# One expert unit of two 64-row halves in plain fp32 in place of two units of 128 rows

## The chip, the cores and the metric

The kernel runs on one core of one Trainium2 chip, in one launch. The metric is the device time of that launch in microseconds (us). A run of a kernel agrees with the next within about 0.3%.

## What is computed

Three layers follow one another; only the second is touched. The attention's output `x` (2304 tokens of 512 numbers) goes to one of eight experts per token, and the result goes through a gated network.

```python
e_idx = np.argmax(x @ w_gate + modality_bias[modality_id], axis=1)
for e in range(8):
    mask = e_idx == e
    h = np.maximum(x[mask] @ w1[e], 0.0)            # 512 -> 1024
    out[mask] = gate_w[mask, None] * (h @ w2[e])    # 1024 -> 512
```

On the reference's own inputs only three experts get tokens: expert 1 gets 48, expert 2 gets 1084 and expert 5 gets 1172. Matmuls keep fp32 accuracy, either as plain fp32 matmuls or as three matmuls of a high and a low part (`hi*hi + hi*lo + lo*hi`) in a type (fp32r) that TensorE streams faster.

## The kernel before

**Stages.** Attention runs first (until about 205 us), then the expert layer in units, then the gated network (from 445.60 us to the end). All engine queues are written out by hand: an engine executes its instructions in the order of the program, and steps of later units are placed between the matmuls of earlier ones.

**Units.** A unit is a set of token rows of one expert. Nine *pair* units (0 to 8, `NA` = 9) of 256 rows come first: two are chosen during the attention (expert 2 twice on these inputs), the other seven by a planner (`Routing.finish`) that counts on the device. What an expert has left, if 128 rows or fewer, goes to *single* units of 128 rows. Here 60 rows of expert 2 and the 48 of expert 1 are left, so units 9 and 10 are singles; both are always in the program. Further singles stand in nested branches (L1848) on the device's count `nb` and aren't taken here.

**The planner.** `finish` compares the counts with the thresholds `thr` on VectorE (L889 to L916), then GpSimd turns the result into the table `tl` (L920 to L940): the expert of each unit, a flag whether it differs from that of the unit before, and `nb`. GpSimd's queue goes on with the scatter of unit 0 (L1212) and the gather of unit 2 (L1105). The sync queue (SP) reads `tl` into registers to address the weight loads.

**Weights.** An expert has eight weight pieces of 512 KB: four column quarters of `w1` (pieces 0, 2, 4, 6) and four row quarters of `w2` (1, 3, 5, 7). Each has one fixed buffer `ws[k]`. `load` (L1122) fills it, and is skipped on the chip where the expert hasn't changed. `high` (L1149, ScalarE) and `low` (L1155, VectorE) split a piece into two fp32r tiles of the pool tag "w" (10 buffers).

**A single unit** (`single`, from L1258) takes 128 rows. `up(q)` makes 256 hidden columns with 12 fp32r matmuls of 256 columns (four chunks of the 512 inputs, three terms; L1272); `turn(q)` transposes them back with two matmuls (L1280) and splits them; `down(q)` adds them to the 512 outputs with six fp32r matmuls of 512 columns (L1288). The plan of eight steps is written out in `plan`. After each step `step` places loads, splits and gathers of the units ahead, and `extra` places work of the gated network: `decode` unpacks its weights (which the inputs hold in a wide format) and stores them to DRAM as `wd`, `early` transposes its first rows (three matmuls, L1525), and `fetch` and `prepare` load and split its first weights.

**Column tiles in the attention.** `Attention.values` (L443) multiplies two heads at once in plain fp32: each matmul has 64 stationary columns, one head writes output partitions 0 to 63 and the other 64 to 127, and the two alternate in the queue.

Of the kernel before, what the change touches and what calls it, by code (L numbers as in the profile page):

```python
# [547 lines left out]
class Routing:  # L548
# [7 lines left out]
    def __init__(self, tc, ctx, keep, xd, ident, mid, w_gate, bias):  # L556
# [10 lines left out]
        self.tl = keep.tile([1, 2 * NU + 1], I32, tag="tl", name="tl")  # L567
# [70 lines left out]
    def tables(self):  # L638
# [24 lines left out]
        self.thr = iota("thr", [P, 2, NA], [[P, 2], [2 * P, NA]])  # L663
# [204 lines left out]
    def finish(self, tmp, ps):  # L868
# [3 lines left out]
        def t(name, shape, dt=F32):  # L872
# [15 lines left out]
        cmp = t("cmp", [P, E, 2, NA])  # L888
        V.tensor_tensor(  # L889
            cmp, cnt.unsqueeze(3).to_broadcast([P, E, 2, NA]), self.thr.unsqueeze(1).to_broadcast([P, E, 2, NA]),  # L890
            ALU.is_gt,
        )
        nu = t("nu", [P, E, 2])
        V.tensor_reduce(nu, cmp, AX.X, ALU.add)
        c = t("c", [P, 2, E])
        V.tensor_copy(c[:, 0], nu[:, :, 1])
        V.tensor_tensor(c[:, 1, ::-1], nu[:, :, 0], nu[:, :, 1], ALU.subtract)
# [9 lines left out]
        V.tensor_scalar(gm, ends, most, None, ALU.min)  # L907
        V.scalar_tensor_tensor(gs, ends, 2.0 * NE, gm, ALU.add, ALU.add)
# [3 lines left out]
            past, self.grp.unsqueeze(2).to_broadcast([P, G, 2 * E]),  # L912
# [3 lines left out]
        V.tensor_reduce(tef, past[0:1], AX.X, ALU.add)  # L916
        yield
        te2 = tef.rearrange("p g o -> p (g o)")
        tl, own, rev = self.tl, t("own", [1, NU]), t("rev", [1, NU])
        g.tensor_copy(own[:, 0:NE], self.te0[:, 0:NE])  # L920
        g.tensor_copy(own[:, NE:NA], te2[:, 2 * NE:2 * NA:2])
        g.tensor_copy(own[:, NA:], te2[:, 2 * NA:])
        g.tensor_scalar(rev, own, -1.0, 2.0 * E - 1, ALU.mult, ALU.add)
        g.tensor_scalar(rev, rev, 0.0, None, ALU.max)
        dif = t("dif", [1, NU])
# [4 lines left out]
        g.tensor_copy(tl[:, 0:NU], own)  # L930
        nb = t("nb", [1, 1])
        g.tensor_scalar(nb, ends[0:1, 2 * E:], float(-2 * (NA - NE)), most[0:1], ALU.add, ALU.add)
        used = t("used", [1, NU])
        g.tensor_scalar(used, self.grp[0:1, 0:NU], float(NA - 1), nb, ALU.subtract, ALU.is_le)
# [5 lines left out]
        g.tensor_copy(tl[:, 2 * NU:], nb)  # L940
# [3 lines left out]
        V.scalar_tensor_tensor(a, gs[:, 0:E], float(P), n0e, ALU.mult, ALU.subtract)  # L944
        V.scalar_tensor_tensor(b, c[:, 0], 2.0 * P, n0e, ALU.mult, ALU.add)
        V.scalar_tensor_tensor(d, c[:, 0], -2.0, gs[:, 2 * E - 1:E - 1:-1], ALU.mult, ALU.add)
# [5 lines left out]
        V.scalar_tensor_tensor(rk, half, float(P), rk, ALU.mult, ALU.add)  # L952
# [17 lines left out]
        V.scalar_tensor_tensor(u[:, 0], gs[:, 0:2 * E], float(-P), co, ALU.mult, ALU.add)  # L970
        V.scalar_tensor_tensor(u[:, 1], gs[:, 0:2 * E], float(P), qf, ALU.mult, ALU.add)
# [17 lines left out]
class Experts:  # L989
# [137 lines left out]
    @staticmethod  # L1127
    def piece(u, p):

        return p if u < NA else (0, 2, 4, 1, 6, 3, 5, 7)[p]  # L1130
# [12 lines left out]
    def high(self, u, p):  # L1143
        k = self.piece(u, p)
        hi = self.w[u, k] = self.part(u, p, "h")
        if (u, p) in self.POOLH:
            self.nc.gpsimd.tensor_scalar(hi, self.ws[k], 1.0, 1.0, ALU.mult, ALU.mult)
        else:
            self.nc.scalar.activation(hi, self.ws[k], AF.Copy)  # L1149

    def low(self, u, p):
        k = self.piece(u, p)
# [6 lines left out]
    def transpose(self, u, c):  # L1159
# [3 lines left out]
        if c == 0:  # L1163
            if u > 1:
# [17 lines left out]
        if u == 1:  # L1182
            if c:
                lo.append(self.ro.wp.tile([P, 2, n], F32R, tag="xg2", name="xl"))
            h, l = hi[c // 2], lo[c // 2]
        else:
            h, l = hi[:, c:c + k], lo[:, c:c + k]
# [70 lines left out]
    def single(self, u, step):  # L1258

        nc = self.nc  # L1260
        xh, xl, _ = self.x[u]
        y = self.ps.tile([P, DM], F32, tag="o", name="y", bufs=1)
        h = {}
        nq = FF // 256

        def up(q):
            wh, wl = self.w[u, 2 * q]
            t = self.ps.tile([P, 2 * P], F32, tag="s", name="h", bufs=SB)
            n = 0
            for c in range(KD):  # L1270
                for a, b in ((xh, wh), (xh, wl), (xl, wh)):
                    nc.tensor.matmul(t, a[:, c, :], b[:, c, :], start=(n == 0), stop=(n == 3 * KD - 1))  # L1272
                    n += 1
            h[q] = self.sp.tile([P, 2 * P], F32, tag="act", name="hr", bufs=5)
            nc.scalar.activation(h[q], t, AF.Copy)

        def turn(q):
# [3 lines left out]
            h[q] = self.relu(t)  # L1281

        def down(q):
            hh, hl = h.pop(q)
            wh, wl = self.w[u, 2 * q + 1]
            for f in range(2):
                for n, (a, b) in enumerate(((hh, wh), (hh, wl), (hl, wh))):
                    nc.tensor.matmul(  # L1288
                        y, a[:, f], b[:, f], start=(q == 0 and f == 0 and n == 0),
                        stop=(q == nq - 1 and f == 1 and n == 2),  # L1290
# [10 lines left out]
    @staticmethod  # L1301
    def ahead(u):

        return u <= NA

    def start(self, u):
        for k in range(8):
            self.load(u, k)
        self.gather(u)
        for p in range(3 + self.ahead(u)):  # L1310
            self.high(u, p)
            if p:
                self.low(u, p - 1)
        for c in range(0, KD, KD // len(self.groups(u))):
            self.transpose(u, c)

    def run(self, units, last, extra):

        for u in units:
            n = u + 1 if u < last else None  # L1320

            def step(f, u=u, n=n):
                for do, a in ((self.low, 2), (self.high, 3)):
                    p = f + a + self.ahead(u)
                    if p < 8:
                        do(u, p)
                    if n is not None and f + a + self.ahead(n) >= 8:
                        do(n, f + a + self.ahead(n) - 8)
                if n is not None:
                    if f == 0:  # L1330
                        if n not in self.g:
                            self.gather(n)
                        self.load(n, self.piece(u, 0))
                        self.load(n, self.piece(u, 1))
                    if f < 6:
                        self.load(n, self.piece(u, f + 2))
# [6 lines left out]
            for _ in (self.pair if u < NA else self.single)(u, step):  # L1343
# [3 lines left out]
class Gated:  # L1347
# [45 lines left out]
    def decode(self, halves=(0, 1)):  # L1393
# [20 lines left out]
        if self.r and (len(self.r) > 1 or not self.todo):  # L1414
# [6 lines left out]
        if self.todo:  # L1421
# [467 lines left out]
```

## Time and profile before

| | us |
|---|---|
| median of 3 runs | 881.71 |
| runs | 881.51 to 881.82 |
| profiled execution, its own time | 881.88 |
| span of its trace | 879.9 |
| TensorE busy in the span | 860.1 |
| VectorE / ScalarE / GpSimd busy | 697.0 / 549.3 / 235.0 |

The span goes from the first to the last instruction, and the profiled execution's own time is 1.98 us longer. In the trace PE is TensorE's matmuls, PEld its weight loads, DVE VectorE, ACT ScalarE, POOL GpSimd and SP the sync engine, of which only the DMA queue matters here. L1272 is line 1272 of the kernel. A matmul's duration contains time in which the next one already runs, so the pace of a series is read from the starts.

### The profile page before, as it was taken

The page shows a single profiled execution, that of the slowest core. Times are in us where ns is not written, and L with a number is a line of the kernel's source. Part 1 is how long each engine was busy: PE and PEld are TensorE (multiplying, and loading weights), DVE is VectorE, ACT ScalarE, POOL GpSimd, SP SyncE. Part 2 cuts the span into 40 slices and gives each one's busy share as a digit, 9 for nine tenths or more (in the row PEclk, how much of TensorE's full clock was granted, in tenths as well). Part 3 has the DMA queues.
Part 4 walks back from the last instruction along what each step waited for, and adds up shares of the span by engine and source line. Part 5 has one row for each costly group of instructions (what it writes and reads, how often), then busy time and mean ns, then how long its engine had stood idle before and what let it go on. Part 6 is the DMA issues. An engine that isn't in the chain of part 4 may idle for free.

```text
span 879.9 us, 16627 instructions
## 1 busy us (share of the span) xinstructions
PE 860.1 (98%) x5536; PEld 747.6 (85%) x5536; DVE 697.0 (79%) x1683; ACT 549.3 (62%) x1190; POOL 235.0 (27%) x482
## 2 busy tenths in 40 slices
PE   7999999999999999999999999999999999999996
PEld 5777767778989999999889988999999999999995
DVE  7677789867989999999789898887666887676751
ACT  7777787774566666667866565556545467545542
POOL 5887876863732222110100000002000002000002
PEclk9999999999999999999999999999999999999998
DMA  7767678964556955579846523234212223321101
GB/s 154 158 146 168 165 170 161 267 152 142 91 157 207 327 175 178 191 235 339 283 148 197 180 85 103 75 106 158 67 64 72 73 73 110 106 72 56 66 1 72
DMA packets 117984, 126.48 MB, mean 144 GB/s; under 512 B 65044, under 2 KB 92200, under 8 KB 117896
## 3 DMA queue, kind: packets, MB, share of 16 engines
q1 hardware_dynamic: 112536, 110.46, 44.1%
q0 software_dynamic: 4640, 14.70, 5.0%
q8 instruction: 44, 0.72, 0.4%
q14 instruction: 44, 0.36, 0.1%
q10 hardware_dynamic: 720, 0.24, 0.1%
HBM read 126.78 MB, written 24.28 MB: 172 GB/s over the span
## 4 chain that ended last, share of the span: by engine, by line
PE 31%; issue 14%; DVE 2%; POOL 1%; ACT 1%; DMA 1%; POOLq 0%; ACTq 0%; DVEq 0%
PE g L1567 20%; PE o L1655 11%; POOL out_dram L1663 1%; PE g L1525 1%; DMA wof<-wd 1%; DVE s L1589 0%; DVE wc L1450 0%; DVE b L1538 0%; DVE ah L1591 0%; DVE x L1554 0%; ACT x L1550 0%; DVE s L1626 0%; ACT pc L1604 0%; DVE wo L1490 0%; POOLq L1884 0%
## 5 line engine op out<-in xcount | busy, mean ns | idle before, releaser
L1567 PE MATMUL g<-x,wc 128*128 128x384 f32 x1524 | 299.1, 338 | 2.8 <-ACT sg L1582 1.2
L1567 PEld LDWEIGHTS g<-x,wc 128*128 128x128 f32 x1524 | 270.6, 188 | 22.6 <-ACT sg L1582 1.5
L1655 PE MATMUL o<-wo,ah 128*128 128x512 f32 x648 | 184.4, 396 | 0.0
L1663 POOL DMA_INDIRECT out_dram<-os,tok x18 | 18.8, 1044 | 408.3 <-ACT os L1662 281.0
L1655 PEld LDWEIGHTS o<-wo,ah 128*128 128x128 f32 x648 | 118.0, 188 | 10.4 <-DVE ah L1591 0.4
L1604 ACT ACTIVATE pc<-g 128x384 f32<-128x384 f32 x102 | 49.9, 489 | 101.0 <-PE g L1567 100.9
L1155 DVE TENSOR_TENSOR wl<-ws,wh 128x1024 fp32r<-128x1024 f32 x76 | 92.2, 1216 | 1.4 <-ACT wh L1149 1.4
L1149 ACT ACTIVATE wh<-ws 128x1024 fp32r<-128x1024 f32 x76 | 80.4, 1061 | 16.3 <-PE y L1242 16.3
L367 ACT ACTIVATE sc<-sc,mn 128x192 f32<-128x192 f32 (+2 forms) x144 | 82.3, 574 | 1.3 <-DVE mn L359 0.8
L299 POOL TENSOR_SCALAR dec<-cum 128x576 f32<-128x576 f32 (+4 forms) x148 | 77.8, 534 | 9.8 <-DMA cum<-drow 5.9
L359 DVE CUSTOM_DVE_ANT_0 sc<-s,dec 128x192 f32<-128x192 f32 (+2 forms) x144 | 58.7, 441 | 20.5 <-POOL dec L299 9.6
L1232 PE MATMUL h<-xh,wh 128*128 128x256 f32 x240 | 69.1, 288 | 0.0
L1232 PE MATMUL h<-xl,wh 128*128 128x256 f32 x240 | 67.8, 283 | 0.0
L1232 PE MATMUL h<-xh,wl 128*128 128x256 f32 x240 | 67.8, 282 | 0.0
L1591 ACT ACTIVATE ah<-s 128x384 fp32r<-128x384 f32 x72 | 37.5, 520 | 43.1 <-DVE s L1589 43.1
L1212 POOL DMA_INDIRECT rows_by_expert<-ys,dst x18 | 21.9, 1214 | 159.1 <-DVE ys L1210 84.6
L350 PE MATMUL s<-qk,qT 64*128 64x320 f32 (+4 forms) x384 | 55.8, 408 | 2.9 <-DVE qk L313 1.6
L1450 DVE TENSOR_TENSOR wc<-wf,wc 128x512 fp32r<-128x512 f32 x72 | 40.2, 560 | 21.3 <-ACT wc L1447 21.3
L350 PEld LDWEIGHTS s<-qk,qT 64*128 64x128 f32 (+1 forms) x384 | 31.2, 177 | 22.6 <-issue 15.8
L1447 ACT ACTIVATE wc<-ws 128x512 fp32r<-128x512 f32 x68 | 42.0, 626 | 10.7 <-DVE ws L1468 8.7
L1242 PE MATMUL y<-wh,hh 128*128 128x512 f32 x120 | 47.6, 397 | 0.7 <-ACT hh L1202 0.7
L1242 PE MATMUL y<-wh,hl 128*128 128x512 f32 x120 | 47.3, 394 | 0.6 <-DVE hl L1203 0.6
(310 smaller groups left out, 1795.8 us busy)
## 6 DMA issues: line engine op xcount, KB each, us to landing
ws<-in_moe_w_dram SPq DMA_DIRECT2D x88, 512.0 KB
wf<-wd SPq DMA_DIRECT2D x36, 512.0 KB
wd<-dec SPq DMA_DIRECT2D x18, 512.0 KB
wof<-wd SPq DMA_DIRECT2D x18, 512.0 KB
cum<-drow SPq DMA_DIRECT2D x15, 576.0 KB
raw<-in_moe_w_gate_dram SPq DMA_DIRECT2D x12, 512.0 KB
raw<-in_moe_w_val_dram SPq DMA_DIRECT2D x12, 512.0 KB
raw<-in_moe_w_out_dram SPq DMA_DIRECT2D x12, 512.0 KB
```

The costliest lines, as they stand in the source:

```text
L299: nc.gpsimd.tensor_scalar(to, c[r, z], -1.0, c[r, a:a + 1], ALU.mult, ALU.add)
L350: nc.tensor.matmul(out[r, o:o + w], q[a, rows], k[a, c:c + w], start=True, stop=True)
L359: nc.vector.tensor_tensor_reduce(s[:, so + c0:so + e], t[j, b, c0][:, 0:e - c0], d[:, do + c0:do + e], -1.0, mn[j][:, 5:6] if c0 else 3.0e ...
L367: nc.scalar.activation(so, so, AF.Exp, bias=mn[j][:, b:b + 1], scale=-1.0, accum_out=sm[:, c:c + 1])
L1149: self.nc.scalar.activation(hi, self.ws[k], AF.Copy)
L1155: eng.tensor_tensor(lo, self.ws[k], hi.bitcast(F32), ALU.subtract)
L1232: nc.tensor.matmul(t, a[:, c, cs], self.chunk(b, c), start=(n == 0), stop=(n == 3 * KD - 1))
L1242: nc.tensor.matmul(y[j], a[:, cs], b[:, f % 2, :], start=(f == 0 and n == 0), stop=(f == nf - 1 and n == 2))
L1447: nc.scalar.activation(t["w"][:, 0, to], of(), AF.Copy)
L1567: self.nc.tensor.matmul(t, p[:, c, :], q[:, c, :], start=(first and n == 0), stop=(n == total - 1), skip_group_check=not first)
L1604: nc.scalar.activation(c, t, AF.Copy)
L1655: nc.tensor.matmul(o[0], x[:, cs], y[:, r, :], start=(o[1] == 0 and k == 0), stop=(o[1] == 2 * self.NP - 1 and k == 2))
```

## The change

Thresholds are now in steps of 64 rows, and what is left of an expert is given out in halves of 64 rows. One unit of 128 rows takes two halves, A on rows 0 to 63 and B on rows 64 to 127, each with an expert of its own. `single` becomes `twin`: each half is a 64-column tile of TensorE, in plain fp32, with no split of weights, inputs or hidden values. The weights of A are read from `ws` itself; those of B come by `load_b` into eight buffers of the tag "w", issued in the last four steps of unit 8. Only unit 9 stands outside the branches; unit 10 and on are taken when `nb`, now in halves, is over 2. `decode` loads no new piece in the last four steps of unit 8 (two are loaded at the end of unit 9 instead), and `fetch` of the gated network's first weights moves from unit 10 to unit 7. The table `tl` gets the experts of the B halves.

```diff
-        self.thr = iota("thr", [P, 2, NA], [[P, 2], [2 * P, NA]])
+        self.thr = iota("thr", [P, 3, NA], [[D, 3], [2 * P, NA]])
+        for j in range(2):
+            nc.gpsimd.iota(
+                self.grp2[D * j:D * (j + 1)], [[2, G]], base=j, channel_multiplier=0, allow_small_or_imprecise_dtypes=True
+            )
...
+        V.tensor_tensor(nu[:, :, 0], nu[:, :, 0], nu[:, :, 1], ALU.add)
+        V.scalar_tensor_tensor(c[:, 1, ::-1], nu[:, :, 2], -2.0, nu[:, :, 0], ALU.mult, ALU.add)
...
+        V.scalar_tensor_tensor(
+            odd, self.grp2[0:1, 2 * NA:].unsqueeze(2).to_broadcast([1, NB, 2 * E]), 1.0,
+            gs[0:1, 1:].unsqueeze(1).to_broadcast([1, NB, 2 * E]), ALU.add, ALU.is_ge,
+        )
+        V.tensor_reduce(teb, odd, AX.X, ALU.add)
...
+        g.tensor_copy(own[:, NU:], teb.rearrange("p g o -> p (g o)"))
...
+        g.tensor_copy(tl[:, 2 * NU + 1:], own[:, NU:])
...
+    def load_b(self, u, k):
+
+        nc, tl = self.nc, self.ro.tl
+        if (u, "b") not in self.e:
+            a = 2 * NU + 1 + u - NA
+            self.e[u, "b"] = nc.sync.value_load(tl[0:1, a:a + 1], min_val=0, max_val=E - 1)
+        e = self.e[u, "b"]
...
+        t = self.wp.tile([P, 1024], F32, tag="w", name="wb", bufs=10).rearrange("p (k f) -> p k f", k=n)
+        nc.sync.dma_start(t, src.rearrange("o (k p) f -> p (o k) f", p=P))
+        self.w[u, k] = self.ws[k].rearrange("p (k f) -> p k f", k=n), t
...
-    def single(self, u, step):
+    def twin(self, u, step):
...
+        side = [slice(D * j, D * (j + 1)) for j in range(2)]
...
             for c in range(KD):
-                for a, b in ((xh, wh), (xh, wl), (xl, wh)):
-                    nc.tensor.matmul(t, a[:, c, :], b[:, c, :], start=(n == 0), stop=(n == 3 * KD - 1))
-                    n += 1
+                for j, r in enumerate(side):
+                    nc.tensor.matmul(t[r], x[:, c, r], w[j][:, c, :], start=(c == 0), stop=(c == KD - 1))
...
-            nc.scalar.activation(h[q], t, AF.Copy)
+            nc.scalar.activation(h[q], t, AF.Relu)
...
-            h[q] = self.relu(t)
+            h[q] = self.sp.tile([P, 2, P], F32, tag="act", name="ht", bufs=5)
+            nc.vector.tensor_copy(h[q], t)
...
             for f in range(2):
-                for n, (a, b) in enumerate(((hh, wh), (hh, wl), (hl, wh))):
+                for j, r in enumerate(side):
                     nc.tensor.matmul(
...
+                        y[r], a[:, f, r], w[j][:, f, :], start=(q == 0 and f == 0), stop=(q == FF // 256 - 1 and f == 1)
...
+    USE = 0, 2, 4, 1, 6, 3, 5, 7
...
+                    if n == NA and f >= 4:
+                        for k in self.USE[2 * f - 8:2 * f - 6]:
+                            self.load_b(n, k)
...
-        ex.run(range(2, NA + 2), NA + 1, extra)
+        ex.run(range(2, NA + 1), NA, extra)
...
-            for u in range(NA + 2, NU):
-                ifs.enter_context(tc.If(nb > u - NA, label="more" if u == NA + 2 else None))
+            for u in range(NA + 1, NU):
+                ifs.enter_context(tc.If(nb > 2 * (u - NA), label="more" if u == NA + 1 else None))
```

Two places show what this makes of the queues. On TensorE, before, around the first `down` of unit 9 (`wh`, `wl` are the weight parts, `xh`, `xl` the inputs, `hh`, `hl` the hidden values):

```order
L1272 MATMUL h<-wh,xh 128x256
L1272 MATMUL h<-wl,xh 128x256
L1272 MATMUL h<-wh,xl 128x256
L1288 MATMUL y<-wh,hh 128x512
L1288 MATMUL y<-wl,hh 128x512
L1288 MATMUL y<-wh,hl 128x512
L1288 MATMUL y<-wh,hh 128x512
L1288 MATMUL y<-wl,hh 128x512
L1288 MATMUL y<-wh,hl 128x512
L1280 MATMUL x<-ident,hr 128x128 x2
```

On TensorE, in the change, the same place (`ws` and `wb` are the weights of halves A and B, L1550 is `early`, L1307 `turn`):

```order
L1300 MATMUL h<-ws_106,x 64x256
L1300 MATMUL h<-wb,x 64x256
L1300 MATMUL h<-ws_106,x 64x256
L1300 MATMUL h<-wb,x 64x256
L1550 MATMUL x<-ident,y 128x128 x3
L1315 MATMUL y<-ws_103,ht 64x512
L1315 MATMUL y<-wb,ht 64x512
L1315 MATMUL y<-ws_103,ht 64x512
L1315 MATMUL y<-wb,ht 64x512
L1307 MATMUL x<-ident,hr 128x128 x2
```

The three terms are gone: two matmuls of 64 rows, one for each half, stand for each chunk. An `up` has 8 of them and a `down` 4.

On the sync queue, before, from step 3 of unit 8 to the first load for unit 10 (`ws_108` and `ws_109` are pieces 6 and 7 of unit 9):

```order
L1385 DMA raw<-in_moe_w_val_dram 128x4x256
...
L1122 DMA ws_108<-in_moe_w_dram 128x4x256
...
L1122 DMA ws_109<-in_moe_w_dram 128x2x512
L1390 DMA raw<-in_moe_w_out_dram 128x1024
L1406 DMA wd<-dec 128x1024
L1390 DMA raw<-in_moe_w_out_dram 128x1024
L1114 TENSOR_LOAD tl
```

On the sync queue, in the change, the same stretch up to the two loads at the end of unit 9:

```order
L1407 DMA raw<-in_moe_w_val_dram 128x4x256
...
L1137 DMA ws_108<-in_moe_w_dram 128x4x256
L1147 TENSOR_LOAD tl
...
L1153 DMA wb<-in_moe_w_dram 128x4x256
...
L1137 DMA ws_109<-in_moe_w_dram 128x2x512
...
L1153 DMA wb<-in_moe_w_dram 128x2x512
...
L1432 DMA wd<-dec 128x1024
L1412 DMA raw<-in_moe_w_out_dram 128x1024 x2
```

Eight loads `wb` of 512 KB (two ahead of `ws_109`, six behind it) now follow one another where the loads of `raw` stood, behind one read of the table.

## Rows read from the trace of the kernel before

**Rows 1.** The page's first part: busy us, share of the span, instructions of TensorE.
```profile
PE 860.1 (98%) x5536; PEld 747.6 (85%) x5536; DVE 697.0 (79%) x1683; ACT 549.3 (62%) x1190; POOL 235.0 (27%) x482
```
**Rows 2.** Stretches in us: PE, PEld, DVE, ACT, POOL busy; granted clock, DMA share, GB/s.
```profile
404.90:415.80 10.90, 10.90 (x71) 9.70 (x70) 10.48 (x26) 9.43 (x19) 0.00 (x0) 1.00 1.07 376
415.80:430.80 15.00, 14.14 (x92) 12.03 (x91) 12.49 (x21) 12.41 (x22) 2.56 (x2) 1.00 0.97 322
```
**Rows 3.** Timeline of PE, units 9 and 10 (start, us, instruction, idle before).
```profile
415.80 0.28 PE L1272 MATMUL h<-wh,xh 128*128 128x256 f32 x1
...
417.12 0.28 PE L1272 MATMUL h<-wh,xl 128*128 128x256 f32 x1
417.24 0.49 PE L1525 MATMUL x<-ident,y 128*128 128x128 f32 x3
...
417.69 0.28 PE L1272 MATMUL h<-wl,xh 128*128 128x256 f32 x1
...
419.00 0.38 PE L1280 MATMUL x<-ident,hr 128*128 128x128 f32 x2
...
419.34 0.28 PE L1272 MATMUL h<-wl,xh 128*128 128x256 f32 x1
...
444.62 0.39 PE L1288 MATMUL y<-wl,hh 128*128 128x512 f32 x1
444.85 0.39 PE L1288 MATMUL y<-wh,hl 128*128 128x512 f32 x1
445.60 6.68 PE L1567 MATMUL g<-x,wc 128*128 128x384 f32 x37 [0.36 <-PEq L1848]
```
**Rows 4.** Timeline of PE in the attention: the column tiles of L443.
```profile
150.79 1.08 PE L443 MATMUL o<-px,vr 128*64 128x512 f32 x4
151.70 0.30 PE L491 MATMUL t<-iw,ot 128*64 128x72 f32 x4
...
152.59 0.60 PE L443 MATMUL o<-pz,vr 128*64 128x256 f32 x4
153.02 0.64 PE L443 MATMUL o<-pw,vr 128*64 128x64 f32 x16
153.48 0.39 PE L443 MATMUL o<-py,vr 128*64 128x128 f32 x4
```
**Rows 5.** Line L443: count, duration in ns (least, median, most).
```profile
L443 PEld LDWEIGHTS o<-pz,vr x64: 136/137/138, 25.3 to 205.2; 128*64 128x64 f32 x64
```
**Rows 6.** Waits on PE, from 445 us: us in total, times, longest.
```profile
PE g L1567 <- ACT sg L1582: 1.2, 1, 1.2
```
**Rows 7.** Timeline of VectorE: a comparison of the planner.
```profile
220.80 0.31 DVE L889 TENSOR_TENSOR cmp<-rk,thr 128x144 f32<-128x144 f32 x1
```
**Rows 8.** Timeline of GpSimd: the planner's table and what follows.
```profile
224.16 0.18 POOL L921 COPY own<-tef 1x7 f32<-1x7 f32 x1 [2.47 <-DVE tef L916]
...
235.44 3.02 POOL L1212 DMA_INDIRECT rows_by_expert<-spare,dst  x1 [0.31 <-DMA ws<-in_moe_w_dram]
238.76 1.00 POOL L1105 DMA_INDIRECT xg<-xd,ids  x1 [0.30 <-DVE ids L775]
```
**Rows 9.** Waits between 195 and 290 us.
```profile
PEld x L1176 <- DMA xg<-xd,ids: 0.3, 1, 0.3
```
**Rows 10.** Timeline of the sync queue, end of unit 7 to the gated network.
```profile
392.58 0.38 SPq L1385 DMA_DIRECT2D raw<-in_moe_w_gate_dram  x1
394.49 3.07 SPq L1122 DMA_DIRECT2D ws<-in_moe_w_dram  x4
...
405.00 2.80 SPq L1122 DMA_DIRECT2D ws<-in_moe_w_dram  x2
...
446.40 0.33 SPq L1479 DMA_DIRECT2D wof<-wd  x1
```
**Rows 11.** Timeline of ScalarE: the user of the load `wof`.
```profile
450.86 1.15 ACT L1487 ACTIVATE wo<-wof 128x512 fp32r<-128x512 f32 x2 [0.30 <-DMA wof<-wd]
```
**Rows 12.** Waits of the sync queue, 360 to 450 us.
```profile
SPq L1385 <- DVE dec L1411: 16.7, 5, 5.4
```

More of the change, by code (lines that the diff above doesn't have):

```diff
@@ L566, in __init__ @@
         self.te0 = keep.tile([1, NE], I32, tag="te0", name="te0")
-        self.tl = keep.tile([1, 2 * NU + 1], I32, tag="tl", name="tl")
+        self.tl = keep.tile([1, 2 * NU + 1 + NB], I32, tag="tl", name="tl")
         self.iw = wp.tile([P, H, 2, D + E], F32, tag="iw", name="iw")
@@ L951, in finish @@
         V.tensor_tensor(rk, rk, wide(a), ALU.add)
-        V.scalar_tensor_tensor(rk, half, float(P), rk, ALU.mult, ALU.add)
+        V.scalar_tensor_tensor(rk, half, float(D), rk, ALU.mult, ALU.add)
         V.tensor_tensor(rk, rk, sel, ALU.mult)
@@ L1143, in high @@
     def high(self, u, p):
-        k = self.piece(u, p)
+        k = p
         hi = self.w[u, k] = self.part(u, p, "h")
@@ L1151, in low @@
     def low(self, u, p):
-        k = self.piece(u, p)
+        k = p
         hi, lo = self.w[u, k], self.part(u, p, "l")
@@ L1299, in single @@
         self.store(u, [y])
-    @staticmethod
-    def ahead(u):
-        return u <= NA
+    USE = 0, 2, 4, 1, 6, 3, 5, 7
     def start(self, u):
-        for k in range(8):
+        for k in self.USE:
             self.load(u, k)
+            self.load_b(u, k)
         self.gather(u)
[L1310 to L1315, printed above, removed]
+        self.transpose(u, 0)
     def run(self, units, last, extra):
@@ L1322, in step @@
             def step(f, u=u, n=n):
[L1323 to L1328, printed above, removed]
+                if u < NA:
+                    for do, a in ((self.low, 3), (self.high, 4)):
+                        if f + a < 8:
+                            do(u, f + a)
+                        elif n < NA:
+                            do(n, f + a - 8)
                 if n is not None:
@@ L1341, in step @@
                 extra(u, f)
-            for _ in (self.pair if u < NA else self.single)(u, step):
+            for _ in (self.pair if u < NA else self.twin)(u, step):
                 pass
@@ L1391, in load, with preload, decode @@
         return r
-    def decode(self, halves=(0, 1)):
+    def preload(self):
+        key, part = self.todo.popleft()
+        self.r.append((key, part, self.load(key, part)))
+    def decode(self, halves=(0, 1), load=True):
         nc = self.nc
@@ L1413, in decode @@
                 self.done.append((key, self.dec.pop(key)))
-        if self.r and (len(self.r) > 1 or not self.todo):
+        if self.r and (len(self.r) > 1 or not self.todo or not load):
             key, part, r = self.r.popleft()
@@ L1420, in decode @@
             self.c.append((o, r, key, part))
-        if self.todo:
-            key, part = self.todo.popleft()
-            self.r.append((key, part, self.load(key, part)))
+        if self.todo and load:
+            self.preload()
     def fetch(self, g):
@@ L1817, in decayed_attention_top1_moe_gated_kernel @@
     with c2:
-        pace, todo = (1, 1, 1, 1, 1, 1, 1, 1), deque((0, 1) * (len(ga.todo) + 1))
         for _ in range(2):
@@ L1824, in extra @@
         def extra(u, f):
-            if u < NA:
-                for _ in range(min(pace[f], len(todo))):
-                    ga.decode((todo.popleft(),))
+            if u < NA or f < 2:
+                ga.decode((f % 2,), u < NA - 1 or u == NA - 1 and f < 4)
+            if u == NA and f in (5, 6):
+                ga.preload()
             if u == NA - 2 and f == 4:
```

89 lines of the change are left out of this document (44 added, 45 removed).

## The prediction

> **What bounds the kernel now.** I read the page's engine shares first: TensorE is busy in 98% of the span [rows 1], so a stretch in which it has less to do is shortened by that, unless something else comes late. Then the stretches around the change: at the end of unit 8 TensorE has no idle time at all, the clock is granted in full (1.00, the 2.4 GHz level), and the DMA engines are full too, at 376 GB/s [rows 2]. That second number matters, for the change needs 4 MB more by an earlier time. In unit 9 TensorE is busy for 14.14 of 15.00 us [rows 2]. The timeline says the rest: unit 9 begins at 415.80, and the gated network's first matmul stands at 445.60 [rows 3]. The two singles take 29.8 us between them, for 108 rows that have something to do.
>
> **What goes.** All of the 29.8 us. For later use, its pieces: eleven starts of fp32r matmuls of 256 columns lie between 415.80 and 417.12, so one costs 0.12 us. The last two of 512 columns start 0.23 apart. An `early` block adds 417.69 - 417.24 - 0.12 = 0.33 us, a `turn` 419.34 - 419.00 - 0.12 = 0.22 us, the change into and out of the transposes included. From the start of the last matmul to the gated network are 0.75 us, of which 0.23 are its own stream and 0.52 the end (the branch among it) [rows 3].
>
> **What comes: the matmuls.** The trace has the same form already, in the attention: 64 stationary columns, plain fp32, two tiles in turn. Each such matmul shows as two MATMUL rows, so the four rows of one line are one pair. A pair of 256 columns takes 153.02 - 152.59 = 0.43 us, a pair of 512 columns up to 151.70 - 150.79 = 0.91 us [rows 4]. An `up` of the twin is four pairs of 256 columns: 4 x 0.43 = 1.72 us. A `down` is two pairs of 512. Twice the row of 256 columns is 0.86, and 0.91 holds the change of tile form as well, which I charge with `turn` and `early`; I take 0.86, so 1.72 us per `down`, and keep 0.91 (0.4 us more in all) for the range. Four of each are 8 x 1.72 = 13.76 us. Four `turn` at 0.22 and four `early` at 0.33 (there were four `early` in the two singles, too) are 2.2. **The twin takes 16.0 us** and ends at 431.8; with the 0.52 behind it the gated network begins at 432.3 instead of 445.60. That is 13.3 us saved.
>
> Against this stands a rule. The rows show weight loads that cost nothing: one load of 64 columns lasts 137 ns [rows 5], four of them would be 0.55 us, and yet a pair takes 0.43; at 64 columns sixteen matmul rows, each with its load, pass in 153.48 - 153.02 = 0.46 us [rows 4]. The Trainium skill, "TensorE: Matmul & The Clock Gate", section "Part 3: Packing small matmuls", says that a weight load overlaps with matmuls in flight only when its row group differs, and column tiles share theirs. By that rule the twin's loads would all stand on top and the sum would be 882.2; the attention's rows don't agree with it (0.43 us a pair, not 0.98).
>
> **Waits in the twin.** `plan` is unchanged: a `turn` never follows its own `up`, and a `down` never its own `turn`, always with at least one block of 1.72 us between, and the copies out of PSUM no longer queue behind splits of weights (those of units 9 and 10 are gone from ScalarE and VectorE). I take 0. The two singles cost 29.8 us where their matmuls and blocks add up to 2 x (48 x 0.12 + 24 x 0.23 + 4 x 0.22) + 4 x 0.33 + 0.52 = 26.2 us [rows 3], so 3.6 us were waits and other small things; half of that, 1.8 us, is the upper bound for one unit.
>
> **Weights of B.** SP issues in order. Unit 9's piece 6 goes out at 405.00, as before; two loads take 2.80 us there with full DMA engines, 1.4 each [rows 10]. Behind it comes a read of the table; from one load to the next with such reads between are 394.49 - 392.58 = 1.9 us at most [rows 10]. A load lands up to 450.86 - 446.40 = 4.5 us after its issue [rows 10, 11]. So the B pieces, in the order of their use (0, 2, 4, 1, 6, 3, 5, 7), with A's piece 7 as the fourth issue, land, from 405.00 + 1.4 + 1.9 + 1.4 + 4.5 on, at 414.2, then 415.6, 418.4, 419.8, 421.2, 422.6, 424.0 and 425.4. The twin needs them at 415.8, 417.9, 419.8, 421.8, 423.8, 426.1, 428.0 and 430.0. The least slack is 1.4 us (piece 4). Their buffers come free in steps 4 to 7 of unit 8, all before 415.80. The loads of `raw` are taken out of these steps for that, and stand at the end of unit 9. I take 0 for the stall.
>
> **Moved work with one answer.** `fetch` moves into unit 7, 1 MB more there, behind stores of `wd` that are units old; `early` and `prepare` stand beside longer matmul blocks on queues that have lost the splits; the two last `raw` loads have over 10 us until their use in the gated network: nothing on the path. If that cover fails, the first gated matmuls wait; they do wait 1.2 us for ScalarE now [rows 6], and I count the loss of that as a bound below, not as a gain.
>
> **The planner.** VectorE gets two operations more on 144 elements and one smaller, and two grow; at 0.31 us for one of 144 elements [rows 7] that is some 0.9 us. GpSimd gets two copies (0.18 us or somewhat more each [rows 8]) and waits for the second of VectorE's: some 0.8 us later. Behind the table GpSimd issues unit 0's scatter, 3.02 us, and right behind it the gather of unit 2 [rows 8]; TensorE's transposes of unit 2 already wait 0.3 us for that gather [rows 9], so the delay isn't hidden there. ScalarE's backlog further on can absorb a part. I take +0.6 us, between 0 and 1.5. Two more small table fills on GpSimd in the attention, while TensorE is busy throughout: 0.
>
> **Sum.** 881.88 (the profiled execution's own time) - 13.3 + 0.6 = 869.2 us. It stands 0.17 above the median of the runs, so **869.0 us** against 881.71.
>
> **Rivals.**
> *B's weights come late.* For it: DMA at 376 GB/s [rows 2], only 1.4 us of slack, and SP's habit of standing still for VectorE's unpacking, up to 5.4 us at a time [rows 12]. Against: those waits belong to `raw` loads, and none stands among the B loads. If one such wait falls ahead of piece 6 anyway, TensorE waits 5.4 - 1.4 = 4.0 us: 873.0.
> *Loads or tiles of TensorE don't overlap.* With the weight loads of 24 pairs (four each, 96 of 137 ns) on top, 13.2 us, the twin takes 29.2 and nothing is gained: 882.2. The attention speaks against it, with the same form; for it, only that the attention never has more than two large pairs in a row.
> *The change doesn't do what it says: a second twin runs.* It decides at more than two halves, that is, with one remainder over 64 rows. The branch then loads 16 pieces that nothing has fetched ahead, 16 x 1.4 = 22.4 us, plus 4.5 for the last to land, 1.7 for its `down` and 0.5: 29 us more, **898 us, slower than before**. Against: the remainders are 60 and 48 rows by the reference's inputs, and the two units between 415.80 and 445.60 agree with that.
>
> **How the numbers follow.** Forecast 0.78, late weights 0.14, no overlap 0.04, second twin 0.03, and 0.01 for something faster still. The range takes the forecast's bounds and the late weights. Low: 868.4 without the planner's 0.6, less 1.2 [rows 6] and less the 0.4 of wait at the branch [rows 3], 866.8. High: 872.9 for late weights, plus 0.4 for the longer `down`, 873.3; the forecast with all its bounds (0.9, 0.4, 1.8) is 872.1 and lies inside. A measurement of this kernel can tell 0.2% (1.8 us) from no change. Faster by more: 0.78 + 0.14 + 0.01, and a quarter of the no-overlap case, in which only a part of the loads shows: 0.94; within: 0.03; slower: 0.03.
>
> **What would show it.** Right: one unit of some 16 us between the last pair unit and the gated network; pairs of L1300 0.43 us and of L1315 0.86 us apart; no wait for DMA at the first use of any `wb`; the planner's gather later by 0.6 to 1 us; the gated network as long as before, 436 us. Wrong: pairs 0.7 us or more apart (weight loads), idle TensorE in front of an `up` or `down` with DMA as the releaser (late weights), a second block of L1300 behind the branch, or a gated network that takes back what was won.

## The result and the profile after

The changed kernel takes **874.47 us** (median of 4 runs, 872.8 to 875.2) against 881.73 beside it: ratio 0.9915, 95% interval 0.9898 to 0.9933. That is 7.3 us faster, or 0.8%. The direction was forecast, but not the size: 12.7 us were expected, and 874.47 lies above the range of 866.8 to 873.3. The profiled execution took 874.48 us with a span of 872.8 us.

The engine shares of the page of the changed kernel:

```profile
PE 852.9 (98%) x5476; PEld 732.8 (84%) x5476; DVE 677.3 (78%) x1661; ACT 529.7 (61%) x1160; POOL 229.0 (26%) x484
```

Against [rows 1] TensorE still fills the span, so what it no longer does has shortened it; ScalarE and VectorE lost work as well. By stretches (us, busy time and count for each engine, granted clock, DMA share, GB/s), the end of unit 8 and the twin up to the first gated matmul:

```profile
404.90:415.80 10.90, 10.90 (x73) 9.78 (x72) 8.00 (x23) 5.87 (x14) 0.00 (x0) 1.00 1.07 367
416.20:437.70 21.50, 19.55 (x117) 8.73 (x116) 8.00 (x18) 7.76 (x17) 2.04 (x3) 1.00 0.79 277
```

Unit 8 is as full as before [rows 2]. The twin's stretch lasts 21.5 us where 16.5 were forecast, and TensorE has gaps in it. The timeline of TensorE shows where (start, duration, engine, line, operation, out<-in, count, and the idle time before with what ended it; L1300 is `up`, L1307 `turn`, L1550 `early`, L1315 `down`, L1592 the first gated matmul). Each matmul of a half shows as two rows; one row of A with one of B is called a pass here:

```profile
416.21 0.65 PE L1300 MATMUL h<-ws,x 128*64 128x256 f32 x2
417.65 0.43 PE L1300 MATMUL h<-wb,x 128*64 128x256 f32 x1 [0.79 <-DMA wb<-in_moe_w_dram]
...
424.60 1.07 PE L1315 MATMUL y<-ws,ht 128*64 128x512 f32 x2
425.22 0.64 PE L1315 MATMUL y<-wb,ht 128*64 128x512 f32 x1
...
435.94 0.59 PE L1315 MATMUL y<-ws,ht 128*64 128x512 f32 x1
435.94 0.59 PE L1315 MATMUL y<-wb,ht 128*64 128x512 f32 x1
437.74 0.44 PE L1592 MATMUL g<-x,wc 128*128 128x384 f32 x1 [1.20 <-ACTq L1870]
```

The reader is to see three things. Expert A's first matmuls run at 416.21, but B's wait for their weights until 417.65. At the first `down` A's first two rows run alone again, ahead of B's. And the first gated matmul, which before followed its branch closely [rows 3], now waits 1.20 us for ScalarE to pass the branch. The issues of SyncE's queue say when B's loads went out:

```profile
404.13 0.81 SPq L1432 DMA_DIRECT2D wd<-dec  x1
405.06 0.38 SPq L1407 DMA_DIRECT2D raw<-in_moe_w_val_dram  x1
405.86 1.49 SPq L1137 DMA_DIRECT2D ws<-in_moe_w_dram  x1
408.22 2.96 SPq L1153 DMA_DIRECT2D wb<-in_moe_w_dram  x2
411.62 1.69 SPq L1137 DMA_DIRECT2D ws<-in_moe_w_dram  x1
413.57 5.75 SPq L1153 DMA_DIRECT2D wb<-in_moe_w_dram  x6
```

B's first piece was issued at 408.22 and had landed only at 417.60: 9.4 us after its issue, where the forecast gave 5.9 (1.4 for the issue and 4.5 for the landing). At 367 GB/s these 9.4 us are 3.4 MB, that is, the piece itself and some five or six transfers of 0.5 MB ahead of it. The Trainium skill, "DMA: Bandwidth & Descriptors", section "Queues, rings and completion order", says that each DMA engine takes descriptors in the order of its ring; the trace agrees, for by its semaphore events the transfers land in the order of their issue, 1.5 us apart here (414.61 and 416.10 for the two ahead, then 417.60).

**Where the time went**, profiled execution against profiled execution (spans 879.9 and 872.8): the stretch from the end of the pair units to the gated network fell from 29.80 to 21.53 us (-8.27), the stretch ahead of it grew by 0.41, and the gated network by 0.76, the last as what is left of the 7.1.

### The profile page after: what moved, and what is told of

It is laid out like the page before. It is cut to its first block, busy times and chain, and to the rows that moved or that the text cites. A ratio compares the mean times of both kernels' runs of the same rounds, so it can differ in the third digit from the quotient of the medians.

```text
span 872.8 us, 16416 instructions
## 1 busy us (share of the span) xinstructions
PE 852.9 (98%) x5476; PEld 732.8 (84%) x5476; DVE 677.3 (78%) x1661; ACT 529.7 (61%) x1160; POOL 229.0 (26%) x484
## 4 chain that ended last, share of the span: by engine, by line
PE 67%; issue 17%; DVE 6%; DMA 3%; POOL 3%; SPq 1%; ACT 1%; POOLq 0%; DVEq 0%; ACTq 0%
PE g L1592 20%; PE o L1680 11%; PE h L1261 10%; PE y L1271 9%; PE s L350 4%; PE o L443 4%; PE t L386 3%; PE t L484 1%; PE t L320 1%; DMA wb<-in_moe_w_dram 1%; DVE spare L1179 1%; PE t L409 1%; PE x L1202 1%; DMA rows_by_expert<-ys,dst 1%; POOL out_dram L1688 1%
## 5 line engine op out<-in xcount | busy, mean ns | idle before, releaser
L1592 PE MATMUL g<-x,wc 128*128 128x384 f32 x1524 | 299.7, 338 | 3.1 <-ACTq L1870 1.2
L1592 PEld LDWEIGHTS g<-x,wc 128*128 128x128 f32 x1524 | 270.9, 188 | 23.8 <-ACTq L1870 2.1
L1179 DVE TENSOR_TENSOR wl<-ws,wh 128x1024 fp32r<-128x1024 f32 x60 | 72.8, 1215 | 1.3 <-ACT wh L1173 1.3
L1173 ACT ACTIVATE wh<-ws 128x1024 fp32r<-128x1024 f32 x60 | 63.4, 1060 | 14.7 <-PE y L1271 14.7
L1241 POOL DMA_INDIRECT rows_by_expert<-ys,dst x17 | 20.0, 1177 | 153.9 <-DVE ys L1239 84.6
```

The costliest lines, as they stand in the source:

```text
L1179: eng.tensor_tensor(lo, self.ws[k], hi.bitcast(F32), ALU.subtract)
L1592: self.nc.tensor.matmul(t, p[:, c, :], q[:, c, :], start=(first and n == 0), stop=(n == total - 1), skip_group_check=not first)
```

## The experiments

Times are medians; the kernel before ran beside each series at 881.5 to 882.0 us. Twelve kernels ran, in five series, each on a chip of its own, so the ratio to the kernel before stands beside each time. Each kernel has one trace.

**The changed kernel again** (no edit).

> The changed kernel once more, unaltered, on the chip on which the others of this series run. Every theory: about 874.5 us, and the same three gaps in the twin: about 1.3 us at its first up for the weights of expert B, 0.5 us at its first down, and 1.2 us at the first gated matmul for ScalarE's passing of the branch. If the scatter of 2.4 us between its runs comes from when the weights land, the profiled execution's first gap grows and shrinks with the time.

874.31 us (873.59 to 876.5), ratio 0.9916 (0.9902 to 0.9929). The profiled execution was the slowest, 876.5, and shows what made this one slow. TensorE's timeline and the stretches of its twin (as above: busy times, granted clock, DMA share, GB/s):

```profile
418.77 0.43 PE L1300 MATMUL h<-wb,x 128*64 128x256 f32 x1 [1.95 <-DMA wb<-in_moe_w_dram]
```
```profile
416.00:418.70 2.70, 0.82 (x4) 0.19 (x2) 1.44 (x5) 2.31 (x5) 0.13 (x1) 1.00 1.08 359
418.70:419.30 0.60, 0.53 (x6) 0.36 (x8) 0.00 (x0) 0.00 (x0) 0.60 (x1) 0.93 1.08 365
419.30:422.90 3.60, 3.60 (x17) 1.83 (x15) 0.00 (x0) 0.43 (x2) 1.20 (x2) 0.54 1.07 365
422.90:426.00 3.10, 3.10 (x28) 1.83 (x28) 2.20 (x4) 1.22 (x3) 0.00 (x0) 1.00 1.06 318
```

B's first piece came 1.1 us later than in the other execution. It took as long to land (9.35 us), but was issued at 409.38 instead of 408.22. Behind that gap the granted clock fell to 0.54, the 1.2 GHz level, for 3.6 us: passes 0.42 us apart instead of 0.215. From the first to the last matmul's start this twin takes 21.91 us, the other 19.73, which is the difference of the two times. A wait for weights is paid twice when the clock falls behind it.

**B's pieces first.** The read of B's entry goes to the start of unit 8, and `load_b` ahead of A's pieces 6 and 7:

```diff
+                    if n == NA and f == 0:
+                        self.read_b(n)
                     if n == NA and f >= 4:
                         for k in self.USE[2 * f - 8:2 * f - 6]:
                             self.load_b(n, k)
+                    if f < 6:
+                        self.load(n, f + 2)
```

> Reads B's entry of the table at the start of unit 8 and issues B's first pieces ahead of A's pieces 6 and 7; nothing else. Theory 'B's first weights were issued too late behind other loads': the two gaps in the twin (1.3 and 0.5 us) go, time falls by 1.3 to 1.9 us, to about 872.8. Rival 'the queue is full, its bandwidth is what is short': some other piece (A's 6 or 7, or a later one of B) is late instead, and the time stays within 0.4 us.

873.39 us (0.9906; 0.9891 to 0.9921): 0.9 less than the changed kernel beside it, half to two thirds of what was expected. The intervals of the two ratios overlap, but the traces agree with it: from the first to the last matmul's start the twin fell from 19.73 to 18.84 us. The gap at the first `down` went and 0.28 us of the first is left (this `up` takes 2.15 us, one without a wait 1.87). The rival was half right, for a new gap stands at the fourth `up`:

```profile
426.64 0.43 PE L1303 MATMUL h<-wb,x 128*64 128x256 f32 x1 [0.23 <-DMA wb<-in_moe_w_dram]
```

**No loads for B.**

```diff
+        if u == NA:
+            t = self.ws[k].rearrange("p (k f) -> p k f", k=n)
+        else:
...
```

> The twin loads nothing for expert B: its second half multiplies A's weights (left out: the eight loads of B's pieces and so B's results). Everything else as in the changed kernel. Theory 'the changed kernel loses 1.8 us and its scatter of 2 us to the loads of B': both gaps for weights go, no stretch of the twin runs at the lower clock, time about 872.5 and runs within 0.5 us of each other. Rival 'the gaps are PE's own (start of column tiles after full-width matmuls)': they stay, and the time stays near 874.4.

872.71 us (872.52 to 873.21; 0.9900, 0.9884 to 0.9915). B's half multiplies A's weights here and its results are left out. No wait for weights is left, the four runs lie within 0.7 us, and from the first to the last matmul's start the twin takes 17.69 us where the changed kernel takes 19.73. **B's loads cost the changed kernel 2.04 us in its profile.** The rest of the miss is TensorE's own: 17.69 and 0.43 for the last pair are 18.1 us, not 16.0.

**Blocks of transposes.** Without waits for weights the starts can be read apart; the run without B's loads:

```profile
416.36 1.95 PE L1303 MATMUL h<-ws,x 128*64 128x256 f32 x16
418.23 0.55 PE L1553 MATMUL x<-ident,y 128*128 128x128 f32 x3
418.71 1.95 PE L1303 MATMUL h<-ws,x 128*64 128x256 f32 x16
420.59 0.44 PE L1310 MATMUL x<-ident,hr 128*128 128x128 f32 x2
420.96 1.95 PE L1303 MATMUL h<-ws,x 128*64 128x256 f32 x16
```

An `up` with an `early` behind it takes 418.71 - 416.36 = 2.35 us, with a `turn` 2.25. In the same run with `early` put directly behind `turn`,

```diff
-        plan = (up, 0), (up, 1), (turn, 0, up, 2), (down, 0, turn, 1), ...
+        plan = (up, 0), (up, 1), (turn, 0, ear, 0, up, 2), (down, 0, turn, 1, ear, 0), ...
```

> No loads for B (as in the run without them; B's results are left out), and the four transposes of gated tokens in the twin put directly behind the turns. Nothing waits for weights here, so only the blocks differ from that run (872.71 us; twin 17.69 us from its first to its last matmul's start, one of the blocks joined already). Theory 'entering and leaving a block costs 0.25 us': three more joins, twin 0.6 to 0.8 us shorter, time 872.0. Rival 'each transpose is dearer': twin within 0.2 us of 17.69.

871.92 us (0.9894; 0.9879 to 0.9909), and its timeline:

```profile
416.33 3.67 PE L1303 MATMUL h<-ws,x 128*64 128x256 f32 x32
419.93 0.44 PE L1310 MATMUL x<-ident,hr 128*128 128x128 f32 x2
420.21 0.49 PE L1554 MATMUL x<-ident,y 128*128 128x128 f32 x3
420.63 1.95 PE L1303 MATMUL h<-ws,x 128*64 128x256 f32 x16
```

From 416.33 to 420.63 are two `up` and the joined block. Behind a block an `up` takes 1.77 us (a first pass of 0.26, seven of 0.215), directly behind another `up` 1.72, so the joined block took 4.30 - 3.49 = 0.81 us. Alone `early` took 2.35 - 1.77 = 0.58 and `turn` 0.48. These are three, two and five transposes: each costs 0.11 us as before, and **each block among column tiles 0.26 us more for entering and leaving it**, with 0.05 in the slower first pass behind it. The twin fell from 17.69 to 16.79 us, 0.30 for each of the three joins, as these prices give: the theory holds, above its bound of 0.25, and the rival falls.

Neighbours in fp32r of full width showed none of it [rows 3]. The twin's neighbours differ from those in two things, plain fp32 and column tiles, and the attention in the trace of before has both beside transposes (L409, L410 and L320 are transposes, L484 plain fp32 of full width, L443 column tiles):

```profile
149.80 0.27 PE L409 MATMUL t<-ident,sc 128*128 128x128 f32 x1
149.91 0.27 PE L410 MATMUL t<-ident,sc 128*128 128x128 f32 x1
150.02 0.41 PE L484 MATMUL t<-iw,ot 128*128 128x144 f32 x2
150.26 0.60 PE L320 MATMUL t<-ident,kr 128*128 128x128 f32 x4
150.79 1.08 PE L443 MATMUL o<-px,vr 128*64 128x512 f32 x4
```

A transpose in front of L484 takes 0.11 us, two L484 take 0.24 (144 of 256 columns at 0.215 are 0.12), so nothing is lost there. The four transposes in front of the column tiles take 0.53 instead of 0.44, that is 0.09 for the way in alone. So the price belongs to the column tiles, not to plain fp32, and it could be read before the change. The Trainium skill, "TensorEngine Tiling (Array Packing)", section "Key Properties", says that a change of tiling mode drains TensorE. It gives no price; these runs do, 0.26 us for the way in and out. That a drain is what takes this time no run here shows.

The same joins (the same edit) in the changed kernel as it is:

> The four pairs of transposes of gated tokens in the twin are put directly behind the transposes of the turns, so that the column-tile matmuls are broken by four blocks instead of eight; as many instructions as before. Theory 'each change between column tiles and full-width transposes costs about 0.25 us by itself': four blocks fewer, 0.8 to 1.2 us less. Rival 'each transpose itself is dearer': no change beyond 0.3 us.

875.98 us (0.9929; 0.9915 to 0.9942), which says nothing of the blocks: in the profiled execution, the slowest, B's first matmul started at 419.38, and 4.1 us at a granted clock of 0.58 followed. And with B's pieces first:

> B's pieces first (as in the run before that moved them), and the four transposes of gated tokens in the twin put directly behind the turns' transposes; to be held against 873.4 us of that run. In its trace one such pair of blocks already stood together and took 0.79 us, where two apart took 0.47 and 0.57. Theory 'a block of transposes costs about 0.25 us for entering and leaving it': three more joins, 0.6 to 0.8 us less in the twin. Rival 'each transpose is dearer': 0, the blocks joined take 1.04 us each.

873.63 us (0.9910; 0.9895 to 0.9925), against 873.39 no gain. The reason can be read: at its first `down` the twin was 0.5 us ahead of the run without the joins, and then it stood at the fourth `up` for the same piece.

```profile
426.66 0.43 PE L1303 MATMUL h<-wb,x 128*64 128x256 f32 x1 [0.35 <-DMA wb<-in_moe_w_dram]
```

**No `early` in the twin**, B's pieces first:

```diff
-            if u == NA - 1 and f >= 4 or u == NA and f in (0, 2, 4, 6):
+            if u == NA - 1:
```

> B's pieces first, and all eight transposes of gated tokens done in unit 8, one a step, none in the twin. Theory 'blocks among column tiles are dear': the twin is 2.0 us shorter (4 x 0.57 less the 0.25 of the one joined), unit 8 longer by 4 x 0.33 = 1.3, together 0.7 us less than 873.4. Rival 'unit 8's ScalarE and VectorE, which split the next weights there, are too full': unit 8 grows by more than 2 us and the time rises.

**872.67 us** (872.01 to 873.82; 0.9900, 0.9885 to 0.9916), 0.7 under 873.39 as expected; the intervals overlap. In the traces the twin's first matmul starts 1.19 us later than with B first, 0.30 for each `early` in unit 8, and the twin is 2.09 shorter. The fourth `up` again stands for its weights, at the same time:

```profile
426.69 0.43 PE L1303 MATMUL h<-wb,x 128*64 128x256 f32 x1 [0.64 <-DMA wb<-in_moe_w_dram]
```

426.64, 426.66 and 426.69, whatever TensorE had done until then: with B first, this piece is set by the transfers.

**The store and the branch.** In the changed kernel the twin's last result is scaled by ScalarE (`ys`, L1240, from 436.61 for 0.69), and ScalarE then passes the branch. Before, the first gated matmul didn't wait for that store: it started at 445.60 [rows 3], and the store ran until 445.96. First the scaling on VectorE, then halved between the two (with B's pieces first):

```diff
+            if u == NA:
+                nc.vector.tensor_scalar(ys[:, 0:DM], y[j], gt[:, j:j + 1], None, ALU.mult)
+            else:
                 nc.scalar.activation(ys[:, 0:DM], y[j], AF.Copy, scale=gt[:, j:j + 1])
```

> The scaling of the twin's result y moves from ScalarE to VectorE, so that ScalarE passes the branch earlier. Theory 'the first gated matmul waits for ScalarE at the branch': the wait of 1.2 us shrinks to about 0.4 and the time falls by 0.6 to 0.9 us. Rival 'the gated network starts no earlier in the end, since its next waits (ScalarE's sg, VectorE's operands) absorb it': the time stays within 0.3 us.

874.73 us (0.9925; 0.9912 to 0.9939), against 874.31 no gain.

```diff
-            nc.scalar.activation(ys[:, 0:DM], y[j], AF.Copy, scale=gt[:, j:j + 1])
+            m = DM // 2 if u == NA else DM
+            nc.scalar.activation(ys[:, 0:m], y[j][:, 0:m], AF.Copy, scale=gt[:, j:j + 1])
+            if u == NA:
+                nc.vector.tensor_scalar(ys[:, m:DM], y[j][:, m:DM], gt[:, j:j + 1], None, ALU.mult)
```

> B's pieces first, and the scaling of the twin's y divided in two halves, one on ScalarE and one on VectorE, so that the later of the two passes the branch about 0.3 us earlier. Theory 'the gated network starts when the last engine that works on the store has passed the branch': the gap of 1.37 us between the twin's last matmul and the first gated one falls to about 1.1, the time by 0.3 us to 873.1. Rival 'the branch itself sets the gap': no change.

875.33 us (0.9924; 0.9911 to 0.9938), 1.9 more than without the halving. The first gated matmuls of the two, and from the second run a stretch and VectorE's half of the store:

```profile
437.60 10.69 PE L1595 MATMUL g<-x,wc 128*128 128x384 f32 x60 [1.50 <-DVEq L1873]
```
```profile
437.32 11.93 PE L1600 MATMUL g<-x,wc 128*128 128x384 f32 x58 [2.02 <-DVEq L1878]
```
```profile
438.70:442.10 3.40, 3.40 (x13) 3.40 (x12) 0.09 (x1) 1.69 (x4) 0.00 (x0) 0.50 0.49 175
```
```profile
435.89 0.48 DVE L1246 TENSOR_SCALAR ys<-y,gt 128x256 f32<-128x256 f32 x1 [0.28 <-ACT ys L1244]
```

The wait moved with the store, from ScalarE's branch to VectorE's. So the releaser is the engine that stores, and not ScalarE as such; but both expectations failed, since VectorE is no quicker through the branch. The second run did not test what it was made for: VectorE's half began only after ScalarE's, and after 2.02 us of waiting the granted clock fell to 0.50 for 3.4 us, so the next 58 matmuls took longer than 60 do in the other. This trace is of the slowest of the five runs; three of the others, up to 875.33, have a mean clock of 0.997 or 0.998, and what made those longer isn't shown. What the gap would be with no store in front of the branch was not tried.

**Relieving the queue.** Ahead of B's pieces lie also a write and a read of the decoding (404.13 and 405.06 above). From the kernel without `early` in the twin, all decoding after unit 8's first two steps moves into the twin, behind B's loads:

```diff
-            if u < NA or f < 2:
-                ga.decode((f % 2,), u < NA - 1 or u == NA - 1 and f < 4)
-            if u == NA and f in (5, 6):
+            if u < NA - 1 or f < 2 or u == NA:
+                ga.decode((f % 2,), u < NA - 1 or u == NA and f < 4)
+            if u == NA and f in (6, 7):
                 ga.preload()
```

> B's pieces first, no transposes of gated tokens in the twin, and the reads and writes of the decoding of gated weights moved from unit 8 into the twin, behind B's loads. In the three runs with B first the piece for the fourth up landed at 426.6 to 426.7 whatever TensorE had done before. Theory 'that is the rate of the transfers, 16 pieces and the decoding's transfers at some 360 GB/s': without 1 MB of the decoding's transfers ahead of them it lands 2 to 3 us earlier, the wait of 0.6 to 0.9 us at the fourth up goes, time 871.8. Rival 'the piece waits for its buffer or for SyncE, not for bandwidth': it lands at 426.7 again, time 872.7.

876.06 us (0.9937; 0.9924 to 0.9951). The theory on the weights holds: TensorE waits for no weights in the twin, the piece for the fourth `up` lands at 421.86 instead of 426.65, and the twin is 1.17 us shorter than without the move. But SyncE came late out of the branch:

```profile
434.78 0.33 SPq L1417 DMA_DIRECT2D raw<-in_moe_w_out_dram  x1
439.82 0.34 SPq L1509 DMA_DIRECT2D wof<-wd  x1
```
```profile
439.68 0.49 ACT L1612 ACTIVATE sg<-g 128x384 f32<-128x384 f32 x1 [5.07 <-SPq L1875]
```

In the changed kernel that first transfer of the gated network is issued at 436.70. Here SyncE's last read stood for its buffer until 434.78, and the program has SyncE wait at the branch until its transfers have landed: by the semaphore events this read landed at 439.16, and SyncE's wait for it ended at 439.17. ScalarE waits for SyncE at the branch, 5.07 us, and the gated network takes 3.9 us longer than in the changed kernel, part of it at the lower clock (0.51 from 450.0 to 453.4). Two gentler forms followed, with two reads and two steps of decoding moved, the second step in the fourth or in the seventh step of the twin:

```diff
+            if u < NA - 1 or u == NA - 1 and f < 6 or u == NA and f < 4:
+                ga.decode((f % 2,), u < NA - 1)
+            if (u, f) in ((NA - 1, 5), (NA - 1, 7), (NA, 4), (NA, 5)):
                 ga.preload()
```

> B's pieces first and no transposes of gated tokens in the twin; of the decoding's transfers the two reads go behind B's first four and behind its last piece, the write behind both, and only two steps of decoding move into the twin, so that SyncE has issued everything by about 426 and reaches the branch about 10 us before the twin ends. Theory 'B's later pieces are late by the rate of the transfers, and the run that moved all decoding lost its gain because SyncE came to the branch at 435.8': the wait at the fourth up is gone or under 0.2 us, the first transfer of the gated network is issued at 436 and not 440, time 871.8. Rival 'any decoding in the twin delays ScalarE and VectorE at the branch': the first gated matmul waits over 1.5 us and the time is above 872.7.

876.75 us (0.9940; 0.9927 to 0.9954). The profiled execution was the fastest of the five, 873.72; what made the others longer, up to 877.96, no trace shows. In it the first transfer was in time (436.30), the wait at the fourth `up` gone, and in its place:

```profile
430.62 0.66 ACT L1450 ACTIVATE dec<-raw 128x512 f32<-128x512 f32 x1 [6.42 <-DMA raw<-in_moe_w_val_dram]
```
```profile
432.12 0.44 PE L1310 MATMUL x<-ident,hr 128*128 128x128 f32 x2 [2.18 <-ACT hr L1305]
```

```diff
-            if u < NA - 1 or u == NA - 1 and f < 6 or u == NA and f < 4:
-                ga.decode((f % 2,), u < NA - 1)
-            if (u, f) in ((NA - 1, 5), (NA - 1, 7), (NA, 4), (NA, 5)):
+            if u < NA - 1 or u == NA - 1 and f < 6 or u == NA and f in (0, 1, 5, 6):
+                ga.decode((int(f in (1, 6)) if u == NA else f % 2,), u < NA - 1)
+            if (u, f) in ((NA - 1, 5), (NA - 1, 7), (NA, 4), (NA, 6)):
                 ga.preload()
```

> As the run with one read moved, but the second of the two decoding steps in the twin comes in its seventh step instead of its fourth, behind ScalarE's last relu, so that no relu stands behind a read that lands at 430.6. Theory 'that run lost its gain only because ScalarE waited 6.4 us for the read, with the fourth relu behind it': the wait of 2.18 us of the fourth turn goes, the time is 871.8, at most 872.4. Rival 'decoding in the twin reaches the branch again (SyncE's last read now waits for a buffer until about 431)': the first gated matmuls wait or the first transfer behind the branch is issued after 438, and the time is above 872.7.

873.91 us (0.9907; 0.9890 to 0.9923). That wait went too, but the rival won. SyncE's last read stood until 433.0 for its buffer and landed at 437.29, SyncE's wait at the branch ended at 437.30, and the first transfer went out at 437.96. Later the gated matmuls waited, and the clock fell (stretch 447 to 457):

```profile
448.37 1.84 PE L1597 MATMUL g<-x,wc 128*128 128x384 f32 x5 [2.14 <-ACT sg L1612]
```
```profile
447.00:457.00 10.00, 8.63 (x40) 8.63 (x41) 8.96 (x21) 6.53 (x15) 0.00 (x0) 0.83 0.42 161
```

The best version with B's results remains the one with B's pieces first and no `early` in the twin, at 872.67 us: under both kernels by its median, though its runs (to 873.82) overlap those of the changed kernel (873.59 to 876.5 in the series run again), and the intervals of the ratios do too.

## Why the prediction was right and wrong

The steps of the sum, each against the profile of the changed kernel; "saved" was forecast at 13.3 and is 8.27.

| step | forecast | measured | read from |
|---|---|---|---|
| eight `up` and `down` | 13.76 | 14.16 | 8 x 1.77 |
| four `turn`, four `early` | 2.2 | 3.96 | 17.69 + 0.43 - 14.16 |
| weights of B | 0 | 2.04 | 19.73 - 17.69 |
| end and branch | 0.52 | 1.37 | 437.74 - 435.94 - 0.43 |
| planner and what else shifts the start | 0.6 | 0.41 | 416.21 - 415.80 |
| gated network longer | 0 | 0.76 | remainder of the spans |

The first four rows add up to 5.05 us of the miss, the last two to 0.57, less 0.3 that lies outside the spans: 5.3, as from 869.2 to 874.48.

- **"Weights of B ... I take 0 for the stall" failed.** The issue time came out right to 0.1 us (408.3 worked out, 408.22 measured), but by luck: A's piece 6 went out at 405.86 and not at 405.00, and the stretch with the read of the table took 0.87 us and not 1.9. The landing did not come out: 9.4 us after the issue instead of 5.9. "A load lands up to 4.5 us after its issue" was read from one transfer in the gated network [rows 10, 11], where the DMA engines have room; here they were full, as [rows 2] showed. The trace of before holds the right price in the same place: A's pieces 6 and 7, issued there at 405.00 and 406.55, landed 10.0 and 9.8 us later by its semaphore events. The rival of late weights named the right effect by another cause (SyncE waiting for VectorE); the 4.0 us it allowed are more than the 2.04 that came. (Its 873.0 stands as 872.9 in the range, a slip that changes nothing.)
- **"Four `turn` at 0.22 and four `early` at 0.33" failed.** These prices came from blocks between fp32r matmuls of full width [rows 3]; among column tiles each block costs 0.26 us more, and 0.05 in the first pass behind it, which over eight blocks is the 0.40 of the table's first row. That 0.91 holds "the change of tile form as well" [rows 4] was a hint that I left for the range, and only with the `down`s.
- **"0.52 the end (the branch among it)" failed.** The change makes the last store the thing that the gated network's start waits for.
- **Right: column tiles overlap.** A pair of 256 columns takes 0.43 us and one of 512 columns 0.86, as forecast, with weight loads of 137 ns under them. The rule quoted from the Trainium skill, "TensorE: Matmul & The Clock Gate", section "Part 3: Packing small matmuls", would have given 882.2; the trace disagrees with it here. The same section excepts a load into a background weight buffer, which the prediction left out; whether that is the case here no run shows.
- **Right: `plan` needs no waits.** Without B's loads TensorE shows no wait between the twin's first and last matmul, so no copy holds a `turn` up. No second twin runs.
- **The planner** was a little dear: unit 2's gather is issued 0.58 us later (239.34 after, 238.76 before [rows 8]), but behind its first transposes, which had waited 0.3 us for it before [rows 9], TensorE's work comes only 0.32 us later, not 0.6.
- **"The gated network as long as before" failed by 0.76**, and I can't say why. The rows of the `o` matmuls show a slow drift, from 8.2 us ahead at the first to 7.5 at the last (after, then before):

```profile
L1680 PE MATMUL o<-wo,ah x648: 386/395/498, 457.0 to 864.5; 128*128 128x512 f32 x162
```
```profile
L1655 PE MATMUL o<-wo,ah x648: 386/393/504, 465.2 to 872.0; 128*128 128x512 f32 x162
```

The median of one is 2 ns longer; from 620 us on no interval between two starts is more than 15 ns longer. The changed kernel run again and the run with B first drift alike. The cause stays open.

## What to carry to other kernels

Price a load's landing by the traffic ahead of it, at the rate of the full queue, and not by a landing seen in a quiet stretch: issue order decides whose weights come late. Price the change of form between column tiles and full-width work per block, and join such blocks. When the last unit before a branch gets shorter, ask which engines still have to pass the branch, SyncE among them, which here leaves it only when its last read has landed: the reads that were moved out of B's way were paid for at the branch twice, and once by ScalarE.

## What was not expected of the hardware

- A wait of 2 us for weights was followed by 3.6 us at a granted clock of 0.54 in which TensorE was busy throughout; a wait of 0.8 us in the other execution of the same kernel was not. Waits of 2.02 us (the halved store) and 2.14 us (the second step later) were followed by such a stretch too, one of 2.18 us (two reads moved) was not, so the length of the wait alone doesn't tell. The changed kernel scatters by 2.9 us in five runs, the kernel before by 0.9 in nine; the mean clock was 0.995 in the run of 876.5 and 0.998 in that of 873.59. Without B's loads one run in eight was long as well (874.39, mean clock 0.996), of which there is no trace.
- SyncE's first transfer behind the branch came 5.0 us after its last one before it (434.78 to 439.82), 4.4 of them until that one had landed, where ScalarE and VectorE needed 0.4 to 1.0 us from the end of the store to the first gated matmul.
